# Where second-layer matmuls may enter a unit of first-layer products: two places in place of seven

## The chip, the cores and the metric

The program runs on one core of one Trainium2 chip. The time is the device time of one execution in microseconds (us). Three runs of the kernel before gave 1176.54, 1179.86 and 1180.22, median 1179.86. The trace comes from one profiled execution on that core.

## The reference

Three stages follow one another. An attention over 2 batches, 8 heads and 576 positions, whose bias is a small network of the distance between two positions, gives 1152 tokens of width 512. A mixture of 8 experts (each 512 to 1024 to 512, ReLU between) adds its experts up with weights `P` that eight rounds of row and column scaling balance. A last feed-forward (512 to 2048 to 512, ELU between) gives the output:

```
for e in range(E):
    h = np.maximum(x @ w1[e], 0.0)
    ye = h @ w2[e]
    out += P[:, e:e + 1] * ye
...
h = x @ w_in
g = np.where(h > 0.0, h, alpha * (np.exp(np.minimum(h, 0.0)) - 1.0))
return (g @ w_out).astype(np.float32)
```

## The kernel before

The two feed-forward stages are worked through as 20 half experts `he`: 0 to 15 are the experts, 16 to 19 the last feed-forward, cut into four. The tokens stand in two column blocks, `n` = 0 with 256 columns and `n` = 1 with 320 (each pair of quadrants folded by a Strassen-like scheme, so that a block product takes seven multiplications in place of eight). One **pass** (`step`) takes one half expert and one block. It runs the first layer of (he, n) and, woven into it, the second layer of the pass before.

**First layer** (`l1`, `product`): a pass has two units of seven products, in the order 1, 4, 2, 5, 6, 3, 7. Product 4 is that of the unit before, so that it comes late. Each product is six matmuls of 256 or 320 columns (tile `m`, or `m3` for product 2), since weights and tokens are each split into a high and a low part and three of the four combinations are taken, over two halves of the depth. Several products add into the same accumulator, and between two of them a copy (`fork`: tiles `p` and `u`) has to be taken by ScalarE, which TensorE waits for. VectorE adds the copies to other accumulators (tiles `c`), and `hidden` turns them into the high and low parts `hh`, `hl` of the hidden layer, with ReLU up to half expert 15 and with a chain of six or seven instructions (ELU) from 16 on.

**Second layer** (`l2`): matmuls of 512 columns into tile `y`, twelve for each output tile of 128 tokens, 48 for block 0 and 60 for block 1. When a tile is done, VectorE adds it to the sum `acc`. Only two accumulators of the kind `psB` are there for `y`.

**What sets the order.** TensorE's order is written out by `step`: after each yield of `l1`, `adv` lets `l2` move on to a share of its matmuls that grows with the products done. Everything else (ScalarE, VectorE, GpSimd, the DMA queue of SyncE) is placed by a planner (`Plan.order`): it goes through the program in a modelled time, gives each engine the operation that can start first there, and among those that can start together the one that is due earliest. A due time follows from the matmuls that need the result. So a new order on TensorE gives new orders on all engines, which then work strictly in the order written.

**Other work on VectorE and ScalarE.** `split1` and `split2` cut the weights of each half expert into high and low parts (tiles `w1h`, `w1l`, `w2h`, `w2l`). `conv` converts the weights of the last feed-forward, which come in 64 bits, in 32 items: a load (`cw`), one instruction on ScalarE (L814), six on VectorE (L817, L824, L829, L834, L837, L842: tiles `ca`, `cb`) and a store (`wsc`). Nothing needs them before half expert 16, but the ELU's first operation waits for all 32 (`after=cv_end`), since its tiles take the space of the conversion's.

**The boundary** is the place between half experts 15 and 16. The sums `acc` of the first stage become the tokens of the second: `x2t` transposes them on TensorE, ScalarE or VectorE copies them out (`xt`), and `ops_build` makes sums `st` and the parts `oh`, `ol` of them, first for block 0, later for block 1. In that stretch the first-layer products of half expert 16 wait for `ol` and for the new `w1l`. Since no product 4 is waiting there, the first unit of each of these two passes has six products.

Of the kernel before, what the change touches and what calls it, by code (L numbers as in the profile page):

```python
# [53 lines left out]
BD_FIN = 6  # L54
BD_FIN0 = 5
L2_OFF = 1
BD_TAIL = 8
BD_LEAD2 = 28
BD_FIN2 = 4
# [161 lines left out]
def attention_moe_elu_ffn_kernel(  # L221
# [160 lines left out]
    def build():  # L382
# [67 lines left out]
        def split1(he, u):  # L450
            if he >= HE or (he, u) in wt:
                return
            t = rawb[1, he, u]
            wt[he, u] = b = [
                buf(f"w1{x}", 2, lambda x=x: wgt.tile([128, 7, 2, 128], F32R, tag=f"w1{x}", name=f"w1{x}")) for x in "hl"
            ]
            st = new_st()
            for i in range(4):
                op(
                    [("D", cD(256))],  # L460
                    lambda e, i=i: w1_sum(t.get(), st.get(), i, eng[e]),
                    r=[(t, 0)] + ([(st, i - 1)] if i in (1, 3) else []) + ([(st, 1)] if i == 3 else []),
                    w=[(st, i)],
                )
            for i in range(4):
                n = 256 if i == 1 else 512
                dst = [slice(0, 2), 2, slice(3, 5), slice(5, 7)][i]
                hi_lo(
                    b, i, lambda x, dst=dst: x[:, dst], lambda i=i: w1_src(t.get(), st.get())[i][1],
                    [(t, 0)] if i < 2 else [(st, 2 * i - 4), (st, 2 * i - 3)], n, alt=he >= 2 * E,  # L470
                )
            load_next()
# [214 lines left out]
        def l1(he, n):  # L687
            for u in range(2):
                x = None
                for i in (1, 4, 2, 5, 6, 3, 7):  # L690
                    if i == 4:
                        if prev[0] is None:
                            continue
                        product(prev[0], 4)
                        evac(prev[0], 4)
                    else:
                        if x is None:
                            x = unit(he, n, u)
                        product(x, i)
                        evac(x, i)  # L700
                    yield i
                prev[0] = x

        def flush():
            product(prev[0], 4)
            evac(prev[0], 4)
            prev[0] = None

        def l2(he, n, order):
            seq = []  # L710
            base = 4 * n
            m = 3 if he >= 2 * E else 2
            seq = [(t, f) for fs in ((0, 1), (2,), (3,)) for t in order[:m] for f in fs]
            seq += [(t, f) for t in order[m:] for f in range(4)]
            ys = {}
            for t, f in seq:
                if t not in ys:
                    ys[t] = misc("y") if m == 3 and t == order[2] else buf("psB", 2, lambda: psB("y"))
                y = ys[t]
                hh, hl = hts[he, n, f]  # L720
                whi, wlo = w2t[he, f]
                c = slice(128 * t, 128 * t + 128)
                N = NN[n]
                hk = [k for k in (0, 1) if 128 * t < N * k + N and 128 * t + 128 > N * k]
                for i, (a, w) in enumerate(((hh, whi), (hh, wlo), (hl, whi))):
                    mm(
                        lambda e, a=a, w=w, f=f, i=i, y=y, c=c: pe.matmul(  # L727
                            y.get(), a.get()[:, c], w.get(), start=(f == 0 and i == 0), stop=(f == 3 and i == 2)
                        ),
                        [(a, kk) for kk in hk] + [(w, 0)], [(y, 0)], 0.233,  # L730
                    )
                    if f == 3 and i == 2:
                        l2_evac(he, base + t, y)
                    yield
# [265 lines left out]
        def step(he, n, ys, ny, lead=0, finish=0, hooks={}, tail=0):  # L1000
            m = 14
            done = 0

            def adv(k):
                nonlocal done
                while done < min(k, ny):
                    next(ys)
                    done += 1

            adv(lead)  # L1010
            for i, _ in enumerate(l1(he, n)):
                o = 0 if lead or he < 2 * E or n else L2_OFF
                adv(lead + round((ny - lead) * max(0, i + 1 - o) / (m - o - finish)))
                for f in hooks.get(i, ()):
                    f()
            adv(ny)
            if not tail:
                for _ in ys:
                    pass
# [16 lines left out]
        for he in range(HE):  # L1036
            for n in range(2):
                if (he, n) in ((0, 0), (2 * E, 1)):
                    continue
                if he == 2 * E and n == 0:  # L1040
                    for t in (0, 2, 1, 3):
                        x2t(t)
                    flush()
                    new_ops(0)
                    ops_build(0, 0)
                    ops_build(0, 1)
                    split1(he, 0)
                    ys = l2(he - 1, 1, order1)
                    step(he, 0, ys, 60 - BD_TAIL, lead=BD_LEAD, finish=BD_FIN, hooks={0: [lambda: split1(he, 1)]}, tail=1)
                    flush()  # L1050
                    for _ in ys:
                        pass
                    for t in (4, 8, 5, 7, 6):
                        x2t(t)
                    new_ops(1)
                    for t in (2, 3, 4):
                        ops_build(1, t)
                    split2(he, 0)
                    split2(he, 1)
                    step(he, 1, l2(he, 0, std[0]), 48, lead=BD_LEAD2, finish=BD_FIN2)  # L1060
                    last = (he, 1)
                    continue
# [9 lines left out]
                ys = l2(*last, od)  # L1072
                fin = BD_FIN0 if (he, n) == (2 * E - 1, 1) else 0
                step(he, n, ys, 60 if last[1] else 48, finish=fin, hooks=hooks)
                last = (he, n)
                if not conved:
# [549 lines left out]
```

## Time and profile before

| | |
|---|---|
| runs, median | 1179.86 us |
| profiled execution: span from its first to its last instruction | 1178.4 us |
| its own time beside the span | not listed on the page; the runs lie from 1.9 below to 1.8 above the span |
| TensorE (PE) busy | 1150.9 us, 98% |
| VectorE (DVE) busy | 910.4 us, 77% |
| ScalarE (ACT) busy | 630.5 us, 54% |
| granted TensorE clock, mean | 0.992 |
| chain that ended last | PE 90%: y (L727) 41%, m (L539) 37% |

Read it like this: an engine is busy where it executes, and PE's matmuls overlap one another, so that the time between the starts of two matmuls, not the duration of one, says how fast it moves. The idle time before an instruction, and what ended it, stands in square brackets.

### The profile page before, as it was taken

How to read it: one execution, taken by the hardware profiler on the slowest of the kernel's cores; microseconds unless marked ns; L12 is line 12 of the kernel's file. 1: busy time of each engine (PE TensorE's matmuls, PEld its weight loads, DVE VectorE, ACT ScalarE, POOL GpSimd, SP SyncE). 2: the span in 40 equal slices, each digit the busy share in tenths (PEclk: the TensorE clock that was granted, in tenths of full speed). 3: DMA queues.
4: the chain of work that ended last, by engine and by line, in shares of the span. 5: the costliest groups of instructions: out<-in, count | busy, mean ns of one | idle time of the engine just before them, and what ended most of it. 6: DMA issues, size and time to landing. Idle time of an engine off the chain costs nothing.

```text
span 1178.4 us, 19626 instructions
## 1 busy us (share of the span) xinstructions
PE 1150.9 (98%) x7432; PEld 1001.2 (85%) x7432; DVE 910.4 (77%) x1936; ACT 630.5 (54%) x1428; POOL 68.0 (6%) x91
## 2 busy tenths in 40 slices
PE   7899999999999999999999999999999998999998
PEld 3467988989888898998988988989889887898987
DVE  7887888845687878878778788787776569888875
ACT  7997677644243344444443444444434347776763
POOL 0102552000000000000000000000000002000000
PEclk8999999999999999999999999999999999999999
DMA  7866631111112233333242333332411101111102
GB/s 212 252 220 213 197 112 49 37 54 55 36 40 96 65 105 91 107 92 105 66 132 68 103 91 107 94 103 70 128 46 54 44 11 51 40 54 37 36 1 81
DMA packets 36286, 104.78 MB, mean 89 GB/s; under 512 B 4065, under 2 KB 4193, under 8 KB 36193
## 3 DMA queue, kind: packets, MB, share of 16 engines
q1 hardware_dynamic: 36192, 103.54, 29.1%
q8 instruction: 58, 0.95, 0.3%
q14 instruction: 36, 0.29, 0.1%
HBM read 81.88 MB, written 21.64 MB: 88 GB/s over the span
## 4 chain that ended last, share of the span: by engine, by line
PE 90%; DVE 3%; ACT 1%; issue 1%; POOL 0%; DVEq 0%; ACTq 0%; POOLq 0%
PE y L727 41%; PE m L539 37%; PE sc L1220 3%; PE av L1302 3%; PE tr L1271 2%; PE bps L1424 1%; PE av L1312 1%; PE av L1299 1%; PE lg L883 0%; PE trl L1283 0%; DVE ol L439 0%; ACT et L1245 0%; PE x2t L977 0%; DVE w2l L439 0%; DVE et L1230 0%
## 5 line engine op out<-in xcount | busy, mean ns | idle before, releaser
L539 PE MATMUL m<-oh,w1h 128*128 128x256 f32 (+1 forms) x1120 | 331.3, 296 | 0.5 <-ACT u L552 0.5
L539 PE MATMUL m<-ol,w1h 128*128 128x256 f32 (+1 forms) x1120 | 330.7, 295 | 0.9 <-DVE ol L439 0.8
L539 PE MATMUL m<-oh,w1l 128*128 128x256 f32 (+1 forms) x1120 | 330.2, 295 | 0.0
L727 PE MATMUL y<-w2h,hh 128*128 128x512 f32 x720 | 284.2, 395 | 3.2 <-ACT hh L646 1.5
L727 PE MATMUL y<-w2l,hh 128*128 128x512 f32 x720 | 283.3, 393 | 0.8 <-DVE w2l L439 0.8
L727 PE MATMUL y<-w2h,hl 128*128 128x512 f32 x720 | 283.8, 394 | 0.0
L539 PEld LDWEIGHTS m<-ol,w1h 128*128 128x128 f32 x1120 | 211.8, 189 | 25.2 <-DVE ol L439 1.1
L539 PEld LDWEIGHTS m<-oh,w1h 128*128 128x128 f32 x1120 | 211.6, 189 | 24.7 <-ACT u L552 1.2
L539 PEld LDWEIGHTS m<-oh,w1l 128*128 128x128 f32 x1120 | 211.7, 189 | 0.1
L727 PEld LDWEIGHTS y<-w2h,hh 128*128 128x128 f32 x720 | 135.2, 188 | 19.0 <-ACT hh L646 2.3
L552 ACT ACTIVATE p<-m 128x256 f32<-128x256 f32 (+1 forms) x160 | 65.8, 411 | 158.6 <-PE m L539 154.5
L727 PEld LDWEIGHTS y<-w2h,hl 128*128 128x128 f32 x720 | 135.2, 188 | 17.6
L727 PEld LDWEIGHTS y<-w2l,hh 128*128 128x128 f32 x720 | 135.3, 188 | 16.3 <-DVE w2l L439 1.4
L552 ACT ACTIVATE u<-m 128x256 f32<-128x256 f32 (+1 forms) x160 | 65.8, 411 | 123.3 <-PE m L539 122.9
L602 ACT ACTIVATE hh<-c 128x512 fp32r<-128x512 f32 (+3 forms) x128 | 72.1, 564 | 104.0 <-DVE c L571 104.0
L758 DVE SCALAR_TENSOR_TENSOR acc<-y,P,acc 128x512 f32<-128x512 f32 x126 | 94.5, 750 | 37.9 <-PE y L727 35.7
L605 DVE SCALAR_TENSOR_TENSOR hl<-c,hh 128x512 fp32r<-128x512 f32 (+3 forms) x128 | 77.5, 606 | 20.3 <-ACT hh L602 18.4
L571 DVE TENSOR_TENSOR c<-m,u 128x256 f32<-128x256 f32 (+1 forms) x80 | 36.6, 457 | 56.7 <-PE m L539 56.1
L1230 DVE CUSTOM_DVE_ANT_0 et<-sc,bt 128x576 f32<-128x576 f32 (+1 forms) x80 | 58.0, 751 | 13.5 <-PE sc L1220 12.2
L1245 ACT ACTIVATE et<-et,nmx 128x576 f32<-128x576 f32 (+1 forms) x80 | 61.6, 775 | 0.2 <-DVE nmx L1230 0.2
L432 ACT ACTIVATE w2h<-raw 128x512 fp32r<-128x512 f32 x80 | 48.6, 626 | 21.5 <-PE y L727 11.8
L439 DVE TENSOR_TENSOR w2l<-raw,w2h 128x512 fp32r<-128x512 f32 x80 | 53.9, 692 | 1.5 <-ACT w2h L432 1.5
(138 smaller groups left out, 1550.0 us busy)
## 6 DMA issues: line engine op xcount, KB each, us to landing
raw<-w1p SPq DMA_DIRECT2D x32, 512.0 KB, 3.7
raw<-w2p SPq DMA_DIRECT2D x32, 512.0 KB, 3.6
scr<-o SPq DMA_DIRECT2D x36, 295.5 KB, 3.0
bt<-scr SPq DMA_DIRECT2D x16, 576.0 KB, 4.4
cw<-w1d SPq DMA_DIRECT2D x16, 512.0 KB, 4.6
wsc<-ca SPq DMA_DIRECT2D x32, 256.0 KB, 4.4
cw<-w2d SPq DMA_DIRECT2D x16, 512.0 KB, 4.4
raw<-wsc SPq DMA_DIRECT2D x16, 512.0 KB, 3.6
```

Source lines behind the costliest of these rows:

```text
L432: act.activation(out=dst(bh.get()), in_=src(), func=ACTF.Copy)
L439: lambda e: eng[e].tensor_tensor(out=dst(bl.get()), in0=src(), in1=dst(bh.get().bitcast(F32)), op=ALU.subtract),
L539: lambda e, w=w, o=o, j=j, k=k: pe.matmul(x["ap"](bank), w.get()[:, ai, j, :], o.get()[:, bi, j, :], start=(k == 0 and i in (1, 2, 5)), st ...
L552: lambda e: act.activation(out=b.get()[:, 0:N], in_=x["ap"](bank), func=ACTF.Copy),
L571: lambda e: eng[e].tensor_tensor(out=blk(b.get()[:, half * N:half * N + N], rev), in0=ap(p), in1=ap(q), op=ALU.add),
L602: op([("A", cA(w))], lambda e: act.activation(out=hh(), in_=ap(), func=ACTF.Relu), r=sk, w=wh, after=gate_)
L605: lambda e: dve.scalar_tensor_tensor(out=bl.get()[:, d], in0=ap(), scalar=0.0, in1=hhf(), op0=ALU.max, op1=ALU.subtract),
L727: lambda e, a=a, w=w, f=f, i=i, y=y, c=c: pe.matmul(y.get(), a.get()[:, c], w.get(), start=(f == 0 and i == 0), stop=(f == 3 and i == 2)),
L758: lambda e: dve.scalar_tensor_tensor(out=a.get(), in0=y.get(), scalar=P[0][:, n, e_:e_ + 1], in1=a.get(), op0=ALU.mult, op1=ALU.add),
L1220: pe.matmul(sc[h][0:r, x, 0:HALF], qs[:, h, qc], w[:, h, kc], start=not last, stop=last)
L1230: dve.tensor_tensor_reduce(out=e.rearrange("p (x j) -> p x j", x=2), in0=sc[0:r, :, 0:HALF], in1=biast[hp, t][0:r, h].rearrange("p (x j) - ...
L1245: act.activation(out=e, in_=e, func=ACTF.Exp, scale=-1.0, bias=nmx[0:r, h:h + 1], accum_out=sm[0:r, h:h + 1])
```

## The change

A tuple `RUNS = (4, 6)` names places in a unit, and `adv` is called only after the products at these places (i counts the yields of `l1` in a pass):

```
+RUNS = (4, 6)
...
             for i, _ in enumerate(l1(he, n)):
                 o = 0 if lead or he < 2 * E or n else L2_OFF
-                adv(lead + round((ny - lead) * max(0, i + 1 - o) / (m - o - finish)))
+                if i % 7 in RUNS:
+                    adv(lead + round((ny - lead) * max(0, i + 1 - o) / (m - o - finish)))
                 for f in hooks.get(i, ()):
                     f()
             adv(ny)
```

The order of the products and of the second-layer matmuls among themselves is the same. In an ordinary pass the second-layer matmuls stood in 14 groups of three to five; now they stand in four: 17, 7, 17, 7 where there are 48, and 21, 9, 21, 9 where there are 60. All instructions but a handful are the same in kind and number; VectorE has 4 fewer, ScalarE 6 more, GpSimd 2 fewer, as the planner gives some of them to another engine.

First TensorE in an ordinary pass over block 1: the end of product 1 of a unit (tile `m_7302`) and what follows it, before.

```order
L539 MATMUL m_7302<-oh1_2988,w1h_6961 128x320
L539 MATMUL m_7302<-ol1_3031,w1h_6961 128x320
L539 MATMUL m_7302<-oh1_2988,w1l_6968 128x320
L727 MATMUL y_7310<-w2h_6748,hh0_7039 128x512
L727 MATMUL y_7310<-w2l_6760,hh0_7039 128x512
L727 MATMUL y_7310<-w2h_6748,hl0_7046 128x512
L539 MATMUL m_7184<-oh1_2988,w1h_6847 128x320
```

The same place after the change (product 1 is `m_7244` here, and product 4 of the unit before is `m_7134`):

```order
L540 MATMUL m_7244<-oh1_2988,w1h_6909 128x320
L540 MATMUL m_7244<-ol1_3032,w1h_6909 128x320
L540 MATMUL m_7244<-oh1_2988,w1l_6921 128x320
L540 MATMUL m_7134<-oh1_2988,w1h_6789 128x320
L540 MATMUL m_7134<-ol1_3032,w1h_6789 128x320
L540 MATMUL m_7134<-oh1_2988,w1l_6800 128x320
```

Three second-layer matmuls stood between products 1 and 4. Now none does; products 1, 4, 2, 5 and 6 follow one another as 30 matmuls, and the second-layer matmuls come behind them.

Then VectorE at the boundary, from the first sum `st` on the new tokens (`xt2`, `xt0`) on, before:

```order
L338 TENSOR_TENSOR st_10785<-xt2_10775,xt0_10760 128x256
L338 TENSOR_TENSOR st_10785<-xt2_10775 128x256
L338 TENSOR_TENSOR st_10785<-xt2_10775,st_10785 128x256
L338 TENSOR_TENSOR st_10785<-xt0_10760,st_10785 128x256
L605 SCALAR_TENSOR_TENSOR hl1_10802<-m_10673,hh1_10781 128x320
L439 TENSOR_TENSOR ol0_10807<-st_10785,oh0_10792 128x4x128
L990 COPY xt1_10817<-x2t_10809 128x512
L439 TENSOR_TENSOR ol0_10807<-st_10785,oh0_10792 128x4x128
L605 SCALAR_TENSOR_TENSOR hl1_10802<-c22_10771,hh1_10781 128x320
L439 TENSOR_TENSOR ol0_10807<-xt0_10760,oh0_10792 128x4x128
L338 TENSOR_TENSOR st_10841<-xt3_10836,xt1_10817 128x256
L338 TENSOR_TENSOR st_10841<-xt3_10836 128x256
```

And after the change, from the same sum on:

```order
L339 TENSOR_TENSOR st_10724<-xt2_10713,xt0_10692 128x256
L339 TENSOR_TENSOR st_10724<-xt2_10713 128x256
L339 TENSOR_TENSOR st_10724<-xt2_10713,st_10724 128x256
L339 TENSOR_TENSOR st_10724<-xt0_10692,st_10724 128x256
L606 SCALAR_TENSOR_TENSOR hl1_10744<-c1_10698,hh1_10721 128x640
L818 SCALAR_TENSOR_TENSOR ca_10736<-ca_10736,cw_10677 128x512
L825 TENSOR_SCALAR cb_10762<-ca_10736 128x512
L830 SCALAR_TENSOR_TENSOR ca_10736<-ca_10736,cb_10762 128x512
L835 TENSOR_SCALAR cb_10762<-ca_10736 128x512
L838 SCALAR_TENSOR_TENSOR cb_10762<-cw_10677,cb_10762 128x512
L843 TENSOR_TENSOR ca_10736<-ca_10736,cb_10762 128x512
L440 TENSOR_TENSOR ol0_10789<-st_10724,oh0_10747 128x4x128 x2
```

A whole item of the weight conversion (L818 to L843) now stands between the first sums and the first `ol`. Before, the last of the 32 items was long done here. In the new order there are two items in each pair of passes where there were three, and eight follow one another at the end: four in the two passes before this sum, and four between it and the last `ol` of block 1. Two of these four stand ahead of the `ol` that the first product of half expert 16 needs. From that sum to the last `ol` of block 1 VectorE had 83 instructions; now it has 109, of which 24 are conversion.

## Rows read from the trace of the kernel before

**Rows 1.** Stretches: window, length; PE, PEld, DVE, ACT, POOL busy; PEclk; DMA; GB/s
```profile
216.00:306.00 90.00, 90.00 (x540) 79.87 (x539) 53.46 (x112) 44.16 (x98) 1.31 (x2) 1.00 0.17 53
400.00:900.00 500.00, 500.00 (x2933) 450.09 (x2932) 395.02 (x740) 212.96 (x452) 0.00 (x0) 1.00 0.31 93
903.00:957.00 54.00, 54.00 (x316) 48.65 (x316) 28.48 (x54) 18.74 (x41) 0.00 (x0) 1.00 0.13 40
959.50:1003.00 43.50, 39.79 (x222) 33.39 (x221) 40.93 (x84) 29.25 (x65) 7.09 (x8) 0.96 0.13 37
997.20:1002.50 5.30, 4.47 (x16) 3.83 (x17) 5.06 (x13) 2.48 (x6) 1.35 (x2) 0.68 0.36 102
1020.00:1159.00 139.00, 139.00 (x814) 124.86 (x812) 113.33 (x227) 96.80 (x214) 5.67 (x5) 1.00 0.13 40
```

**Rows 2.** Timeline of PE, ends of four long runs: start, duration, line, names, shape
```profile
952.51 0.30 PE L539 MATMUL m<-oh,w1h 128*128 128x320 f32 x1
...
956.76 0.31 PE L539 MATMUL m<-oh,w1l 128*128 128x320 f32 x1
...
959.57 0.39 PE L727 MATMUL y<-w2h,hh 128*128 128x512 f32 x1
...
961.86 0.49 PE L977 MATMUL x2t<-csb,acc 128*128 128x128 f32 x3
...
979.51 0.28 PE L539 MATMUL m<-oh,w1h 128*128 128x256 f32 x1
...
981.51 0.28 PE L539 MATMUL m<-oh,w1l 128*128 128x256 f32 x1
...
1161.89 0.39 PE L727 MATMUL y<-w2h,hl 128*128 128x512 f32 x1
...
1173.23 0.39 PE L727 MATMUL y<-w2l,hh 128*128 128x512 f32 x1
```

**Rows 3.** Timeline of PE and ACT in an ordinary pass: a product's end and its copy
```profile
510.53 0.31 PE L539 MATMUL m<-oh,w1l 128*128 128x320 f32 x1
...
510.93 0.44 ACT L552 ACTIVATE p<-m 128x320 f32<-128x320 f32 x1
```

**Rows 4.** Timeline of DVE, conversion items in the middle, and the last one
```profile
735.37 0.70 DVE L817 SCALAR_TENSOR_TENSOR ca<-ca,cw 128x512 f32<-128x512 f32 x1
...
738.16 0.42 DVE L824 TENSOR_SCALAR cb<-ca 128x512 int32<-128x512 int32 x1
...
740.53 0.69 DVE L842 TENSOR_TENSOR ca<-ca,cb 128x512 f32<-128x512 f32 x1
...
870.33 0.69 DVE L842 TENSOR_TENSOR ca<-ca,cb 128x512 f32<-128x512 f32 x1
```

**Rows 5.** Timeline of DVE at the boundary: first sum, last ol of block 1
```profile
959.52 0.43 DVE L338 TENSOR_TENSOR st<-xt,xt 128x256 f32<-128x256 f32 x1 [0.53 <-ACT xt L988]
...
1002.62 0.42 DVE L439 TENSOR_TENSOR ol<-st,oh 128x256 fp32r<-128x256 f32 x1
```

**Rows 6.** Timeline of PE at the boundary: its waits, and the next half expert's start
```profile
958.20 0.66 PE L977 MATMUL x2t<-csb,acc 128*128 128x128 f32 x4 [0.69 <-ACT xt L988]
...
997.22 0.42 PE L539 MATMUL m<-ol,w1h 128*128 128x320 f32 x1 [0.78 <-DVE ol L439]
...
999.03 0.74 PE L727 MATMUL y<-w2l,hh 128*128 128x512 f32 x1 [0.81 <-DVE w2l L439]
...
1004.85 0.50 PE L727 MATMUL y<-w2h,hh 128*128 128x512 f32 x1 [1.08 <-ACT hh L646]
...
1017.20 0.28 PE L539 MATMUL m<-oh,w1h 128*128 128x256 f32 x1
```

**Rows 7.** Timeline of DVE and PE in the first pass over block 1
```profile
221.29 0.41 DVE L439 TENSOR_TENSOR ol<-st,oh 128x256 fp32r<-128x256 f32 x1
...
222.23 0.31 PE L539 MATMUL m<-oh,w1h 128*128 128x320 f32 x1
```

More of the change, by code (lines that the diff above doesn't have):

```diff
@@ L56 @@
 L2_OFF = 1
+RUNS = (4, 6)
 BD_TAIL = 8
@@ L1012, in step @@
                 o = 0 if lead or he < 2 * E or n else L2_OFF
-                adv(lead + round((ny - lead) * max(0, i + 1 - o) / (m - o - finish)))
+                if i % 7 in RUNS:
+                    adv(lead + round((ny - lead) * max(0, i + 1 - o) / (m - o - finish)))
                 for f in hooks.get(i, ()):
```

## The prediction

> **What bounds the kernel now.** I read the busy time by stretches first, then TensorE's waits, then the timeline at the places that the new order touches. From 400 to 900 us PE is busy 500.00 of 500 at a granted clock of 1.00 while DVE has 395.02 [rows 1]; from 1020 to 1159 PE again has no gap. There only PE's own pace counts: a wait that another engine loses or gains there is worth nothing until it reaches PE. The boundary between half experts 15 and 16 is different: from 959.5 to 1003.0 DVE is busy 40.93 of 43.50 us and PE 39.79 [rows 1], and PE's waits end with DVE or with ScalarE, which itself waits for DVE's results: 0.78 for `ol`, 0.81 for `w2l`, 1.08 for `hh` [rows 6]. In that stretch DVE sets the time. So the change has two prices: what it does to PE's pace in the gapless stretches, and what it does to DVE's queue at the boundary.
>
> **PE's pace: 3.6 us less.** The order says that the second-layer groups of an ordinary pass go from 14 to four. What a group costs beside a pure run comes out of the long runs in rows 2. A `y` run takes 11.34 us for 50 steps (1161.89 to 1173.23), 0.2268 each; `m` with 320 columns 4.25 for 29 steps (952.51 to 956.76), 0.1466; `m` with 256 columns 2.00 for 17 steps (979.51 to 981.51), 0.1176. A pair of passes (both blocks) has 108 `y`, 84 and 84 `m`, 276 matmuls: 24.49 + 12.31 + 9.88 = 46.68 us at these steps. The stretch from 400 to 900 has 2933 matmuls in 500 us [rows 1], so that a pair takes 47.05. The 28 groups of a pair cost 0.37 together. A group of ten, 959.57 to 961.86 [rows 2], takes 2.29 against 2.27, so that a long group still costs 0.02; eight of them in a pair make 0.18. That saves 0.19 a pair. Woven passes lie from 216 to 957 and from 1018 to 1159, 883 us or 18.8 pairs: 3.6 us. It can't be under 0, unless a new wait comes (below), nor over 6.9, which is the whole surcharge of 18.8 pairs.
>
> The Trainium skill speaks against any saving here: TensorE: Matmul & The Clock Gate, section "Wait — 56ns, not 53.3ns?", gives the start-to-start of warm matmuls as N ÷ 2.4 GHz plus about 2.5 ns, whatever stands before, 215.8 ns for 512 columns. By that the 28 groups cost nothing and the term is 0. Rows 2 show about 11 ns more than it for each of the three shapes, and a pair in the woven stretch is 0.37 us slower than the pure runs, so that I take the rows.
>
> **The waits inside a unit: 0.** Product 6 overwrites what product 1 left, so PE waits there for ScalarE's copy. Products 4, 2 and 5 used to stand between with three groups of `y`; now the three stand alone, 19 steps or 2.2 us in block 0. The copy ends at 511.37, 0.84 us after product 1's last matmul starts at 510.53 [rows 3]. What hides it is 18 matmuls; the cover would be gone if the copy stood 1.4 us behind other work in ScalarE's queue. The other two such places get more room than before, as 17 or 21 `y` now stand between products 6 and 3. Accumulators for `y`: the third tile needs the first one's, 12 `m` and 3 `y` later, about 2.1 us, where it had one product and three or four `y`.
>
> **The boundary: 11.8 us more.** In the new order four conversion items lie between the first sum on the new tokens and the last `ol` of block 1; in the trace the last item ends at 871.0, 88 us ahead of that sum [rows 4, 5]. The price of an item: 738.16 to 740.53 for its four middle instructions, which follow one another, 0.69 for the last, 0.70 for the first [rows 4], and a step of 0.04 at each end: 3.8 us, four of them 15.3. Beside them the stretch has two instructions more, about 0.7 each: 1.4. DVE's work there grows from 40.9 to 57.6 us. The stretch, now 43.5 us, becomes 57.6 if DVE never idles and 60.2 if it idles as it does now: 14.1 to 16.7 more. Two things are given back. First, PE transposes the first new tile ten matmuls earlier, so that the wait of 0.69 before the second tile's transposes [rows 6] goes: 1.0. Second, PE has less left once the last `ol` is there: before, ten products and 15 `y` from 1004.85 on, so that the next half expert starts at 1017.20 [rows 6], 14.2 after the last `ol`; now the first five products stand ahead of the `y`, so that eight products (0.88 each) and 15 `y` remain, 10.4, behind some 1.1 us of DVE work on `hl`: 11.5, which is 2.7 less. So 10.4 to 13.0; I take 11.8, as DVE's idle time is partly filled. The four items before it fall into the passes of half expert 15, where DVE has 28.48 of 54 us [rows 1]: with 15.3 more it is at 81%, like the middle at 79%, where PE has no gap: 0.
>
> Lower bound of this term: 0 would need the 24 instructions to lie beside PE work. PE's products of half expert 16 need `ol` and `w1l` that stand behind them in DVE's queue, and rows 6 show PE waiting for such parts already without them. Upper bound: 16.7, and 1 us more if an item waits for its load.
>
> **TensorE's clock: 1.0 more.** In rows 1 the granted clock is 0.68 from 997.2 to 1002.5, a mixture of its two levels, after PE had waited three times. Longer waits will bring the lower level (1.2 GHz) more often. Most of it lies beside DVE's work; what doesn't is 30 matmuls of 320 columns behind the last wait, 4.4 us at full clock and 8.0 at half at most. 0 to 3.6; I take 1.0.
>
> **The first pass over block 1: 0.7 more.** Product 5 started at 222.23, 0.5 us after its last `ol` was ready at 221.70 [rows 7]. Ten `y` that stood before it (2.3 us) now stand behind, so PE can wait up to 1.8 there. One `w2l` and one `hl` that stood ahead of that `ol` now stand behind it (about 1.1). DVE has 53.46 of 90 us in that stretch [rows 1], so that nothing else suffers. 0 to 1.8; I take 0.7.
>
> The sum: −3.6 + 11.8 + 1.0 + 0.7 = +9.9 on the profiled execution's span of 1178.4, so 1188.3. The median of the runs is 1.4 above that span, for what lies around it, which stays: 1189.8.
>
> **The rivals.**
> - *The deferred conversion is hidden (faster or equal).* Place: the boundary. Its price falls below what the pace gives once no more than one of the four items (3.8 us) lies on the path, as when sums and `ol` are ready so early that PE's 30 `y` in advance and the transposes, some 9 us, cover the rest. For it: ScalarE and GpSimd have room there (29.25 and 7.09 of 43.5, rows 1). Against it: DVE's order is fixed, two whole items stand ahead of the `ol` of the very first product, and DVE is busy for 94% of the stretch. With no item on the path the time is 1179.8 − 3.6 + 0.7 = 1177; with one or two 1181 to 1184.
> - *Grouping gains nothing*, since the pace of a matmul would not depend on its neighbours: the pace term is 0 and the rest stays: 1193.4. Against it: the 0.37 us of a pair.
> - *The copies come late.* If ScalarE's queue brings product 1's copy 0.15 us after product 6 could start, in each of 75 units, that is 11 us more, 1201. It decides from a lateness of 1.4 us on; rows 3 show a copy that starts 0.40 after the last matmul's start and no backlog. ScalarE is busy 43% from 400 to 900.
>
> **How the numbers follow.** This kernel's measurement tells about 0.3%, 3.5 us, from no change. Chances: the forecast 0.72 (own range 1184 to 1195), grouping gains nothing 0.10, copies late 0.05, hidden conversion 0.13, of which 0.06 end faster and 0.07 within 0.3%. So slower 0.87. The range: the term for the boundary with its ends (10.4 to 16.7), the clock's 0 to 3.6, the first pass's 0 to 1.8, the pace's 0 to −6.9 give 1183 to 1202 if all ends meet; I leave out the top, which needs all bounds at once, and take 1183 to 1197.
>
> **What would show it.** In the new profile: PE without gaps from 400 to 900 with more matmuls in it (about 2945); two conversion items in a pair of passes; from the first sum on new tokens to the last `ol` 57 us or more with DVE at over 94%; PE's waits there longer by some 13 us, ended by DVE's `ol` and `w1l`; the start of half expert 17 about 12 us further from the last product of half expert 15. Wrong: PE gaps in the middle ended by ScalarE's `p`, or a boundary of under 50 us.

## The result, and the profile after

The changed kernel takes 1190.43 us (median of six runs, 1188.61 to 1192.88); the kernel before, beside it on the same chip, 1180.04 (six runs, 1176.54 to 1180.80). The ratio is 1.0096, with an interval of 1.0079 to 1.0112: slower, by more than the 0.3% that a measurement tells from no change. (The ratios, here and below, are not the quotients of the medians; they differ from those by up to 0.2%.) 1189.8 was forecast, with a range of 1183 to 1197.

The profiled execution has a span of 1186.8 us, against 1178.4. Its stretches, in the columns of [rows 1]; the fourth reaches from the first sum on the new tokens to the last `ol` of block 1, as the fourth of [rows 1] does, and the two after it lie inside it:

```profile
216.00:306.00 90.00, 89.84 (x541) 80.58 (x540) 51.52 (x109) 42.67 (x98) 1.26 (x2) 1.00 0.17 53
400.00:900.00 500.00, 500.00 (x2944) 452.71 (x2943) 359.69 (x693) 204.60 (x451) 0.00 (x0) 1.00 0.25 80
903.00:957.00 54.00, 53.68 (x318) 48.08 (x316) 41.69 (x79) 23.06 (x49) 0.00 (x0) 1.00 0.32 103
955.00:1014.15 59.15, 46.15 (x230) 37.54 (x229) 55.53 (x110) 34.16 (x72) 5.28 (x7) 0.88 0.24 73
964.50:968.30 3.80, 3.80 (x10) 2.85 (x9) 3.54 (x7) 1.01 (x2) 0.00 (x0) 0.50 0.01 5
973.00:976.80 3.80, 3.80 (x22) 3.80 (x21) 3.31 (x9) 1.97 (x4) 0.00 (x0) 0.55 0.52 163
```

Two things are to be seen. From 400 to 900 us, the middle, PE has no gap and executes 2944 matmuls where it had 2933: it has become faster there. DVE has less to do in it, 359.69 us where it had 395.02, and more just before and in the boundary: 41.69 where 28.48 was, and 55.53 in a stretch of 59.15 where it had 40.93 in 43.50.

How far the kernel has come is read from the start of the same product in both. First the start of half expert 15's pass over block 1 and that of half expert 17's, on PE, in the kernel before, and then in the changed one:

```profile
933.70 0.30 PE L539 MATMUL m<-oh,w1h 128*128 128x320 f32 x1
...
1041.56 0.31 PE L539 MATMUL m<-oh,w1h 128*128 128x320 f32 x1
```

```profile
929.80 0.30 PE L540 MATMUL m<-oh,w1h 128*128 128x320 f32 x1
...
1050.48 0.30 PE L540 MATMUL m<-oh,w1h 128*128 128x320 f32 x1
```

At the first place the changed kernel is 3.90 us ahead, at the second 8.92 behind. The stretch between them has grown by 12.8, and all of the loss lies there.

What DVE does there (timeline of DVE, the counterpart of [rows 5] and of the item in [rows 4]):

```profile
955.01 0.43 DVE L339 TENSOR_TENSOR st<-xt,xt 128x256 f32<-128x256 f32 x1
...
957.22 0.69 DVE L818 SCALAR_TENSOR_TENSOR ca<-ca,cw 128x512 f32<-128x512 f32 x1
...
960.32 0.69 DVE L843 TENSOR_TENSOR ca<-ca,cb 128x512 f32<-128x512 f32 x1
960.93 1.28 DVE L440 TENSOR_TENSOR ol<-st,oh 128x512 fp32r<-128x512 f32 x2
...
969.07 0.69 DVE L843 TENSOR_TENSOR ca<-ca,cb 128x512 f32<-128x512 f32 x1
...
978.40 0.68 DVE L843 TENSOR_TENSOR ca<-ca,cb 128x512 f32<-128x512 f32 x1
...
988.46 0.69 DVE L843 TENSOR_TENSOR ca<-ca,cb 128x512 f32<-128x512 f32 x1
...
1013.74 0.42 DVE L440 TENSOR_TENSOR ol<-st,oh 128x256 fp32r<-128x256 f32 x1
```

Four conversion items end in it, at 961, 970, 979 and 989. The first stands from 957.22 to 960.93, 3.71 us, ahead of the `ol` that the first product needs.

And what PE waits for there (timeline of PE, the counterpart of [rows 6]; the first row is the last matmul of product 7 in half expert 15's last unit, the last row the start of half expert 17):

```profile
953.60 0.31 PE L540 MATMUL m<-oh,w1l 128*128 128x320 f32 x1
...
963.87 0.80 PE L728 MATMUL y<-w2h,hl 128*128 128x512 f32 x1 [2.73 <-DVE hl L606]
...
972.54 0.39 PE L540 MATMUL m<-ol,w1h 128*128 128x256 f32 x1 [2.97 <-DVE ol L440]
...
978.54 0.39 PE L540 MATMUL m<-oh,w1l 128*128 128x256 f32 x1 [1.26 <-DVE w1l L440]
...
998.03 0.50 PE L728 MATMUL y<-w2h,hh 128*128 128x512 f32 x1 [2.06 <-ACT hh L647]
...
1006.24 0.50 PE L728 MATMUL y<-w2h,hh 128*128 128x512 f32 x1 [1.82 <-ACT hh L647]
...
1008.26 0.63 PE L728 MATMUL y<-w2h,hl 128*128 128x512 f32 x1
1008.69 0.63 PE L728 MATMUL y<-w2h,hh 128*128 128x512 f32 x1
...
1026.66 0.28 PE L540 MATMUL m<-oh,w1h 128*128 128x256 f32 x1
```

Before, no wait there was longer than 1.08; now the longest two are 2.97 and 2.73, and both end with a result that stood behind an item in DVE's queue. After them PE runs at the lower level of its clock: 0.50 from 964.5 to 968.3 and 0.55 from 973.0 to 976.8, and later steps of 0.43 (1008.26 to 1008.69) where a `y` else takes 0.227.

### The profile page after: what moved, and what is told of

Read it like the earlier page. It is cut to its first block, busy times and chain, and to the rows that moved or that the text cites. A ratio compares the mean times of both kernels' runs of the same rounds, so it can differ in the third digit from the quotient of the medians.

```text
span 1186.8 us, 19631 instructions
## 1 busy us (share of the span) xinstructions
PE 1151.3 (97%) x7432; PEld 1002.3 (84%) x7432; DVE 897.8 (76%) x1932; ACT 625.0 (53%) x1434; POOL 64.5 (5%) x89
## 4 chain that ended last, share of the span: by engine, by line
PE 85%; DVE 6%; ACT 2%; issue 1%; DMA 1%; POOL 0%; ACTq 0%; DVEq 0%; POOLq 0%
PE y L728 40%; PE m L540 35%; PE sc L1222 3%; PE av L1304 3%; PE tr L1273 2%; PE bps L1426 1%; DMA wsc<-ca 1%; PE av L1314 1%; DVE st L339 1%; PE av L1301 1%; DVE ol L440 0%; ACT et L1247 0%; PE lg L884 0%; DVE w2l L440 0%; PE trl L1285 0%
## 5 line engine op out<-in xcount | busy, mean ns | idle before, releaser
L540 PEld LDWEIGHTS m<-ol,w1h 128*128 128x128 f32 x1120 | 211.0, 188 | 10.4 <-DVE ol L440 3.8
```

Source lines behind the costliest of these rows:

```text
L540: lambda e, w=w, o=o, j=j, k=k: pe.matmul(x["ap"](bank), w.get()[:, ai, j, :], o.get()[:, bi, j, :], start=(k == 0 and i in (1, 2, 5)), st ...
```

## The experiments

The leading theory (A in the expectations): the loss is DVE time of the deferred conversion items at the boundary, some 3.8 us each, and the grouping by itself gains. Its rivals are that the grouping itself costs at the boundary, that the items only delay the start of the ELU, which waits for the last of them, and, from the prediction, that grouping is worth nothing. The runs undo or add one of the two parts at a time: the items' place in time, and the grouping in ordinary or in boundary passes. "Boundary" below is the time from the start of half expert 15's second pass to the start of half expert 17's, as above, less that of the kernel before (107.86 us). Medians of the kernel before in these runs were 1179.2 to 1179.7.

**The change with its items back in time.** Each item gets a due time in the planner's terms, and the planner's due time `l` of an operation takes the smaller one:

```
+CV_D0, CV_DD = 175.0, 15.5
...
+            l = min(l, o.due)
...
-   ... r=[kb], w=[ka])
+   ... r=[kb], w=[ka], due=CV_D0 + CV_DD * len(wscw))
```

> The changed kernel, but each of the 32 conversion items has a due time of its own in the planner, so that three of them stand in a pair of passes again and the last ends well ahead of the boundary. Theory A (the four deferred items in VectorE's queue at the boundary cost the time): the boundary's 11.8 us go, the pace's 3.6 stay, 1177 us (1175 to 1180). Theory B (the boundary passes lose because their own second-layer matmuls come in two groups in place of many): nothing changes, 1188 to 1191.

Measured: 1174.52, ratio 0.9968 (0.9955 to 0.9980). It is faster than both kernels, and just below theory A's 1175 to 1180, since the grouping turns out to gain in the boundary passes too (below). Its middle and the stretch from sum to `ol` (windows, columns of [rows 1]):

```profile
400.00:900.00 500.00, 500.00 (x2944) 452.51 (x2943) 385.73 (x741) 207.78 (x453) 0.00 (x0) 1.00 0.30 93
958.92:1001.89 42.97, 39.63 (x235) 34.04 (x235) 40.10 (x81) 30.68 (x70) 10.05 (x11) 1.00 0.09 26
```

and the end of its last item on DVE:

```profile
861.24 0.68 DVE L845 TENSOR_TENSOR ca<-ca,cb 128x512 f32<-128x512 f32 x1
```

The matmuls in the middle stay at 2944, and the boundary is 3.8 us shorter than before instead of 12.8 longer. The grouping is kept here, so it is not what costs. Against the changed kernel's ratio, four items make 1.28%, 15.1 us.

**The due times alone**, as a control, with the second-layer matmuls in 14 places as before (the diff above without `RUNS`).

> The kernel before with the due times of the conversion items alone; the second-layer matmuls stay in 14 groups. It is the control for the kernels that have due times and grouping together. Theory A (an item costs only where it stands between the first sum on the new tokens and the last ol of block 1): no item stands there in either kernel, so nothing changes: 1179.6, within 1.2 us (ratio 0.999 to 1.001), stretch from sum to ol 43 to 43.6 us, PE 2933 matmuls from 400 to 900. Rival: the due times by themselves gain what was put down to grouping in the kernel with due times (1174.5): then 1176 or less, and grouping is worth only the rest.

Measured: 1178.45, ratio 0.9995 (0.9980 to 1.0010): no change, and 2931 matmuls from 400 to 900. PE's order is that of the kernel before, matmul for matmul. Its middle and its stretch from sum to `ol` (windows):

```profile
400.00:900.00 500.00, 500.00 (x2931) 450.07 (x2930) 389.23 (x735) 212.37 (x453) 0.00 (x0) 1.00 0.29 92
958.38:1001.68 43.30, 39.00 (x225) 32.45 (x223) 40.87 (x84) 29.91 (x67) 7.08 (x8) 1.00 0.13 37
```

What the kernel with due times gains over this one is the grouping's.

**The items late, without the grouping.** In the kernel before, each load of an item is held back to the time at which the changed kernel has it (times of the planner's model):

```
+CV_AT = [109.0, 171.0, 198.0, ... 759.0, 768.0, 779.0]
...
-                    w=[(w, 0)], after=attn_end, ready=CV_T0,
+                    w=[(w, 0)], after=attn_end, ready=max(CV_T0, CV_AT[len(wscw)]),
```

> The kernel before with all its 14 places, but each conversion item's load is held back until about the time at which the changed kernel ran it, so that four items stand behind the first sum on the new tokens. Theory A: it loses what the boundary costs without the gain of the pace, 1192 us (1189 to 1195). Theory B: 1180, as before.

Measured: 1193.99, ratio 1.0138 (1.0116 to 1.0161), boundary 16.1 longer. The stretch from sum to `ol`, and two waits of PE in it (window; timeline):

```profile
958.51:1018.62 60.11, 45.86 (x217) 36.91 (x216) 53.93 (x105) 32.31 (x69) 9.37 (x10) 0.83 0.25 79
```

```profile
966.68 0.50 PE L728 MATMUL y<-w2h,hl 128*128 128x512 f32 x1 [3.56 <-DVE hl L606]
...
982.14 0.58 PE L540 MATMUL m<-oh,w1l 128*128 128x256 f32 x1 [3.02 <-DVE w1l L440]
```

Nearly the same length, the same kind of waits, a low clock again, without any grouping. The late items are enough for the loss.

**Two items late in place of four.** Loads and due times 20 us apart (`CV_D0, CV_DD = 166.0, 20.0`, `ready=max(CV_T0, CV_D0 - 16 + CV_DD * len(wscw))`), otherwise the kernel before.

> The kernel before with its 14 places, its conversion items spread evenly so that two of them, not four, stand behind the first sum on the new tokens; the last one ends as far into the boundary as with four. Theory A (each late item takes its own time in VectorE's queue): half of what four cost, about 8 us more than before, 1188 us (1185 to 1191). Theory C (the end of the last item sets the time, since the ELU's first operation waits for it): nearly as much as with four, 1192 to 1195.

Measured: 1186.46, ratio 1.0057 (1.0036 to 1.0079), boundary 5.9 longer. The stretch (window), and the end of the last item on DVE in this run, then in the one with four late items:

```profile
957.02:1007.44 50.42, 41.85 (x225) 33.88 (x223) 46.70 (x96) 31.05 (x69) 7.20 (x8) 0.97 0.20 63
```

```profile
980.99 0.69 DVE L844 TENSOR_TENSOR ca<-ca,cb 128x512 f32<-128x512 f32 x1
```

```profile
992.16 0.69 DVE L843 TENSOR_TENSOR ca<-ca,cb 128x512 f32<-128x512 f32 x1
```

With 12 conversion instructions in it, two items, the stretch is 50.42 where it was 43.50 and, with four, 60.11. The loss grows with the number of items: 6.7 us by the ratio for two, 16.3 for four, about 3.4 and 4.1 each, alike within their intervals.

The run was meant to hold the end of the last item fixed, so as to test the gate of the ELU, and it doesn't: that end lies 24.7 us behind the first sum, and 34.3 with four items. Number and lateness fall together here, so that the totals leave theory C standing. What speaks against it is DVE's own time. From the kernel before to two and to four late items the stretch grows by 6.9 and 16.6, and DVE's busy time in it by 5.8 and 13.0 (40.93, 46.70, 53.93); in the changed kernel by 14.6 of 15.7. A gate by itself would let DVE idle and give it no work. So the items' work makes most of the growth, and at most the 1.15, 3.61 and 1.05 us by which DVE idles more can be the gate's. That it holds the ELU back is seen: its first instruction starts at 986.21 with two items and at 997.50 with four, 4.5 and 4.7 us after the last item's end. No run takes it away, so that its share of those few us stays open.

**Grouping in all but the boundary passes, items late** (`if i % 7 in RUNS or he == 2 * E:` around `adv`, in the changed kernel).

> The changed kernel, but the two boundary passes (half expert 16) take second-layer matmuls in after every product, as before; the conversion stays late. Theory A: within 2 us of the changed kernel, 1188 to 1192. Theory B: the loss goes, 1176 to 1180.

Measured: 1192.29, ratio 1.0127 (1.0105 to 1.0148). Giving the boundary its 14 places back doesn't help; the time is 0.3 us above theory A's range and 0.3% above the changed kernel, with overlapping intervals.

**Grouping in the boundary passes alone** (`or he != 2 * E`), where the items end in time by themselves.

> The kernel before, with the grouping at two places only in the two boundary passes (half expert 16); all other passes have 14 places and the conversion is where it was. Theory A: 1180 (1178.5 to 1182). Theory B: 1188 to 1191.

Measured: 1177.27, ratio 0.9978 (0.9962 to 0.9993), boundary 4.0 shorter, 2930 matmuls in the middle.

```profile
955.78:998.71 42.93, 39.37 (x235) 34.11 (x235) 40.73 (x81) 30.79 (x70) 9.26 (x11) 1.00 0.10 26
```

PE executes 235 matmuls in the stretch where it had 222, at a clock of 1.00 where it had 0.96. The time is below theory A's range, which put the grouping at nothing here: it gains at the boundary. The control has the clock of 1.00 too, executes 225, and its boundary is 1.5 us shorter (106.34) than in the profile of before, so that some 2.5 of the 4.0 are the grouping's.

**Grouping in the ordinary passes alone, items in time** (due times as above, and `or he == 2 * E`).

> As the first experiment (due times), but with all 14 places in the two boundary passes: what remains of the change is the grouping in ordinary passes. By the step of 0.19 us a pair: 3 us less than before, 1176.7 (1175 to 1178.5), and so some 2 to 4 us more than the first experiment, if the grouping in the boundary passes is worth what its run alone gave. If the two are not additive: 1174.5.

Measured: 1176.88, ratio 0.9985 (0.9969 to 1.0000). In the median a gain of 2.6 us, whose interval reaches no change. The profile says it more sharply: 2946 matmuls in the middle, and from the first pass of half expert 3 to the second of half expert 15 it is 2.39 us shorter than before, to the digit what the changed kernel gains there.

**Grouping from half expert 3 on, items in time** (`or he < 3`): it leaves the first passes and the balancing, where the changed kernel has two new waits, as they were.

> As the first experiment (due times), but with all 14 places in the passes of the first three half experts, where the changed order brought a wait of 0.32 us for the first products of block 1 and one of 1.14 for an accumulator behind the balancing of the weights. If these two waits are the price of the grouping there, 0.5 to 1.5 us less than the first experiment: 1173.5. If they come from somewhere else: 1175.

Measured: 1174.37, ratio 0.9952 (0.9935 to 0.9968), which can't be told from the first kernel here (0.9968). The waits of the first passes are gone and so is the pace gained there. This one and the first are the fastest.

**One place in place of two, items in time** (`RUNS = (6,)` and the due times): all second-layer matmuls behind product 7, so that none stands between a product and the copy of it that the next needs.

> As the first experiment (due times for the conversion), but with one group of second-layer matmuls in a unit in place of two, behind product 7, so that products 5, 6, 3, 7 follow one another. If a copy must be ready seven steps after the last matmul it waits for (0.82 us in block 0, 1.03 in block 1) and takes 0.76 to 0.85 until it is done, PE waits in block 0 at two places of a unit: 3 to 12 us more than the first experiment, 1178 to 1186. If the copies stay hidden, the four groups fewer in a pair give another 1.7 us: 1173.

Measured: 1182.19, ratio 1.0024 (1.0006 to 1.0041). The middle, the one kind of wait that is seen in it, and a copy on ScalarE with the product that comes behind it (windows; timeline of PE; of ACT; of PE):

```profile
400.00:900.00 500.00, 497.95 (x2905) 446.99 (x2905) 387.23 (x737) 207.18 (x449) 0.00 (x0) 1.00 0.30 91
```

```profile
407.55 0.50 PE L730 MATMUL y<-w2h,hh 128*128 128x512 f32 x1 [0.16 <-DVE acc L761]
```

```profile
412.04 0.39 ACT L555 ACTIVATE p<-m 128x256 f32<-128x256 f32 x1 [1.03 <-PE m L542]
```

```profile
412.48 0.38 PE L542 MATMUL m<-oh,w1h 128*128 128x256 f32 x1
412.70 0.28 PE L542 MATMUL m<-ol,w1h 128*128 128x256 f32 x1
```

The middle loses: 2905 matmuls. The copy ends at 412.43 and the product starts at 412.48; its first step is 0.22 instead of 0.12, some 0.1 us, three times in a pair of passes. And a run of `y` this long overtakes DVE: once in a pair the third tile waits for `acc` to free its accumulator (0.32 and 0.11 above the usual in the two steps). The time lies in the expected range, but more of the loss is this second wait, which the expectation didn't name, than the copies' 0.3 us a pair. So the cover of the copies can be used up: two places keep it (in the changed kernel no step from 400 to 900 is more than 0.06 us above the usual one of its shape), one doesn't.

By the ratios the parts add up within their intervals. Ordinary grouping −0.15%, boundary grouping −0.22%, both measured together −0.32%. Items late +1.38%; with all grouping that makes 1.06%, measured 0.96%; with ordinary grouping 1.23%, measured 1.27%. Each of these has about ±0.2%.

## Why the prediction was right

**PE's pace** (−3.6, 0.19 a pair): measured 0.19 a pair. The lead of the changed kernel grows from 1.51 us at half expert 3's first pass to 3.90 at half expert 15's second, 2.39 in 12.5 pairs, and 2945 matmuls were expected in the middle, 2944 came. So the surcharge of a group is real: with 20 groups fewer a pair gets back 0.19 of its 0.37 us. The rule of the Trainium skill that was weighed (TensorE: Matmul & The Clock Gate, "Wait — 56ns, not 53.3ns?"), by which nothing would be gained, does not fit here, and the rival that grouping gains nothing falls with it. That page of the Trainium skill gives its rule for matmuls back to back; that it holds whatever stands before is the prediction's reading of it. Nor do all three shapes lie about 11 ns above that rule, as the prediction says: for 256 columns an estimate by the formula of that page of the Trainium skill is 109.2 ns, and 117.6 was read, 8 more.

The lead at half expert 3 is not part of this gain. At the first pass over block 1, before any group has moved, the changed kernel is already 1.79 us ahead (start of that pass on PE, before, then after):

```profile
217.34 0.31 PE L539 MATMUL m<-oh,w1h 128*128 128x320 f32 x1
```

```profile
215.55 0.31 PE L540 MATMUL m<-oh,w1h 128*128 128x320 f32 x1
```

Five of the runs above have the order of the kernel before on every engine up to there, and start this pass between 3.0 us earlier and 3.4 later than it: it is what executions differ by in the attention.

**The waits inside a unit** (0): PE is busy for 500.00 of 500. Product 1's last matmul, the start of product 6, the 17 `y` that now stand together and the start of product 3 (timeline of PE), then product 1's copy (of ACT; compare [rows 3]):

```profile
508.37 0.31 PE L540 MATMUL m<-oh,w1l 128*128 128x320 f32 x1
...
510.95 0.31 PE L540 MATMUL m<-oh,w1h 128*128 128x320 f32 x1
...
511.83 0.39 PE L728 MATMUL y<-w2h,hh 128*128 128x512 f32 x1
...
512.99 0.39 PE L728 MATMUL y<-w2h,hl 128*128 128x512 f32 x1
...
515.71 0.30 PE L540 MATMUL m<-oh,w1h 128*128 128x320 f32 x1
```

```profile
508.77 0.44 ACT L553 ACTIVATE p<-m 128x320 f32<-128x320 f32 x1 [1.22 <-PE m L540]
```

The copy starts 0.40 after the matmul's start and takes 0.44, as before. It ends at 509.21, 1.74 ahead of product 6.

**The boundary** (+11.8, and the clock +1.0): +12.8 measured for the two. By its steps: an item 3.71 (3.8 said), the stretch 59.15 (57.6 to 60.2 said), DVE busy in 94% of it. Within that, DVE's work is 55.53 where 57.6 was said, and its idle time 3.62 where at most 2.6 was said: 2.0 us of it are waits for an item's own step on ScalarE, which in turn waits 1.7 for the store of an earlier item. The first sum comes 1.41 us after the start of the last matmul of product 7 in half expert 15's last unit, 955.01 against 953.60, where it was 2.76 behind (959.52 against 956.76): 1.35 given back, 1.0 said. From the end of the last `ol` to half expert 17 it is 12.5, where it was 14.2: 1.7 given back, 2.7 said. The missing 1.0 is the clock, which was put down apart: behind the last wait seven `y` take 0.43 instead of 0.23, 1.4 us. The two other times of low clock lie where DVE is busy anyway. What no run separates is how much the clock costs in them.

So the mechanism is the one forecast, but the equality of the sums, 12.8 and 12.8, is in part luck: the errors of the steps cancel, and the profile of before has a low clock of its own in this place, without which (the control) the growth would be 14.3.

Two details were off. PE's waits in the stretch were to grow by some 13 us; PE's idle time there grows by 9.3 (3.71 to 13.00), and its busy time by 6.4 for eight matmuls more, at a clock of 0.88 where it was 0.96. And waits ended by `ol` and `w1l` were announced; one of the two longest ends with `hl`, and two of about 2 us with ScalarE's `hh`, which itself comes late behind DVE. Whatever DVE hands to PE is late there, and not just the operands of the products. The four items before the boundary were costed at nothing, with DVE at 81%: it is at 77%, and PE idles 0.32 of 54 us.

**The first pass over block 1** (+0.7): the wait came, and smaller. PE, without a gap from 216 to 306 before, has 89.84 of 90 there, and this is the place (timeline of PE):

```profile
217.99 0.31 PE L540 MATMUL m<-oh,w1h 128*128 128x320 f32 x1
218.46 0.41 PE L540 MATMUL m<-ol,w1h 128*128 128x320 f32 x1 [0.16 <-DVE ol L440]
218.71 0.31 PE L540 MATMUL m<-oh,w1l 128*128 128x320 f32 x1
```

Two steps of 0.47 and 0.25 where 0.147 is usual: 0.4 us. Not foreseen was about 0.6 at the balancing, where the first `y` of a run waits 0.98 for `acc` (timeline of PE); such a wait was 0.33 before.

```profile
335.76 0.50 PE L728 MATMUL y<-w2h,hh 128*128 128x512 f32 x1 [0.98 <-DVE acc L759]
```

Added up: −3.6 + 0.4 + 0.6 + 12.8 = 10.2; the medians differ by 10.4. The two profiled spans differ by 8.4 only, as the changed kernel's starts out 1.8 ahead. The prediction's step of 1.4 from the span to the median was not only "what lies around" the span: every run listed with its span is some 1.8 longer than it, which puts the profiled execution of the kernel before at 1180.2, a little above the median. The hidden conversion, the main rival on the other side, fell on what spoke against it: DVE was busy in 94% of that stretch before anything was added, and a fixed order leaves little room to slip into.

What stays open: why the planner, given the grouped order, takes two items in a pair where it took three. The due times restore the three, so it is its choice among operations that are not urgent; the runs here don't say which of its rules decides. Nor is the 2.5 us that boundary grouping gains split into the earlier transposes, the fewer products left behind the last `ol`, and the waits.

## What to carry to other kernels

When a change alters only the order on one engine, read where the scheduler put the work that nothing waits for: here 24 instructions, the last of them moved by 118 us (870.33 to 988.46) into a stretch of 43 us that their engine bounds, cost four times what the change gained. Work without a due time may drift to the place where it is in the way; here a due time kept it out. And a time that a change loses may hide a gain: kept apart, the two parts of this one give 1174.5 us, faster than either kernel.

## What the runs showed of the hardware

Two things were not expected. A run of `y` behind products starts slowly: in the changed kernel, from 511.83 to 512.99 five steps take 0.232 each, and the twelve from there to 515.71 0.227, so that the surcharge of this group, 0.02 us, lies in its first five matmuls. And the clock doesn't follow from the waits alone. In the kernel before, waits of 0.69, 0.78, 0.81 and 1.08 [rows 6] came with 0.68 in a stretch of 5.3 us [rows 1]. The control, with PE's order of before, has the waits 0.69, 0.79, 0.81 and 1.08 at the same places, stays at 1.00 and has a boundary 1.5 us shorter (its stretch of 5.3 us, window; two of the waits, timeline of PE):

```profile
996.09:1001.39 5.30, 4.18 (x22) 3.40 (x22) 5.23 (x14) 2.89 (x8) 1.35 (x2) 1.00 0.34 102
```

```profile
996.09 0.41 PE L541 MATMUL m<-ol,w1h 128*128 128x320 f32 x1 [0.79 <-DVE ol L441]
...
997.90 0.50 PE L729 MATMUL y<-w2l,hh 128*128 128x512 f32 x1 [0.81 <-DVE w2l L441]
```

Part of what two executions of one order differ by is such a stretch; what brings it in one and not in the other, these runs don't show.
